# Wide query-key products for two blocks, values ahead of the second softmax, and outputs added by accumulating DMA, in a fused attention and gated-MLP layer

## The chip, the cores and the metric

The kernel runs on one core of a Trainium2 chip. Such a core has five engines with an instruction queue each: TensorE (PE in the profile) for matrix products, VectorE (DVE), ScalarE (ACT), GpSimd (POOL) and SyncE (SP). Each engine works through its instructions in order, and engines wait for each other by semaphores. SP's queue carries nearly all transfers here; GpSimd issues those that add to their destination. PSUM, where matmul results land, has eight banks of 128 x 512 fp32. The metric is the time of one execution on the device in microseconds (us), the median over runs.

## The reference

```python
B, S, D = 1, 2048, 640;  H = 32;  Dh = 20;  W, dil = 8, 2;  F = 1536
xn = _layernorm(x)
qkv = xn @ wqkv                                   # q, k, v: 32 heads of 20
idx = pos[:, None] - off[None, :]                 # off = 0, 2, ... 14
logits = jnp.einsum("bhsd,bhswd->bhsw", q, kg) * scale     # 8 keys per query
logits = jnp.where(mask[None, None, :, :], logits, -1e9)
attn = _softmax(logits, axis=-1)
o = jnp.einsum("bhsw,bhswd->bhsd", attn, vg)
h = (xn @ w_gate) * (xn @ w_up)                   # no activation between
return x + o.reshape(B, S, D) @ wo + h @ w_down
```

All inputs and the output are bf16. The two branches, attention over eight dilated positions and the gated product, read the same normalised x.

## The kernel before

The 2048 rows are 16 tiles of 128 for the layer norm (`front`) and four blocks of 512, j = 0 to 3, for everything else. D = 640 is five chunks of 128, F = 1536 is twelve. The normalised x is kept transposed (XNT), by TensorE for the first four tiles and by transposing DMA for the others.

Projections (L655, L687) give q (QT) and k (KT) with channels on partitions, and v, which is stored to DRAM (`v_scratch`) and read back shifted. A chunk of 128 channels holds four channels of each of the 32 heads.

Query-key products: for a block, DVE multiplies q with eight shifted views of k. `narrow` does four shifts of one chunk in one instruction (128 x 2048 bf16, L819) into a slot PRD. TensorE then sums over the channels of a head with a 0/1 matrix G, four 32-column matmuls per slot (L930, in `logits`), ten slots per block: two halves of the shifts (r = 1, 0) times five chunks. For a block in `QUAD`, four of the five chunks go another way (`wide`): DVE multiplies q straight from PSUM with two shifts of one chunk in fp32 (128 x 1024, L864), and the four chunks are added before TensorE sees them. Of those additions (`sum32`, `close`), the ones in `BY_DMA` are DMAs that GpSimd issues with an add at the destination (L886, 512 KB in SBUF), the others are GpSimd's own (L890, L908). Then four slots go to TensorE instead of ten. Before the change only block 3 is in `QUAD`.

Softmax runs for two blocks at a time (`softmax(x)`, x = 0 for blocks 0 and 1, x = 1 for 2 and 3) on DVE and ScalarE; its last step is L981. Then SP moves the result in 16 small DMAs (32 partitions of 4 x 256 B each, `move`) to ATX, where partitions are the channels of a chunk.

Weighted values: 20 units (block, chunk). For a block, ScalarE first copies two parts of ATX to two PSUM banks (L1076, `at_copy`). A unit's shifted v comes as four DMAs into one of four buffers VX; DVE multiplies VX with the two banks (L1091, fp32, slots PV), GpSimd adds pairs (L1096), TensorE sums the rest with a 0/1 matrix SEL (L1144) in batches of units (`BATCH`), and ScalarE evacuates to OT.

Gated product: for block j and each of 12 steps m, TensorE makes gate and up in two PSUM banks (L1195, five matmuls each), ScalarE copies the gate to SBUF (L660, tiles HT, HX or XNT), and DVE multiplies with up from PSUM (L1204), or ScalarE copies up too (UX) and GpSimd multiplies (L1221). A gate's bank is free once ScalarE has copied it.

Down and output: per tile of 128 rows two pieces of 320 columns, 12 matmuls over F and 5 over the attention's channels (L1277); DVE adds x (XR, loaded again) and writes FOUT (L1290), which SP stores.

The order is not written by hand. Each of these steps is a Python generator that yields tasks and conditions, and `Sched` places them greedily by its own durations: each engine's instruction order is fixed when the program is built, with a priority per task, a count of free PSUM banks, and waits only on the data itself. `calm` keeps GpSimd's additions out of the time in which a softmax runs on DVE.

Of the kernel before, what the change touches and what calls it, by code (L numbers as in the profile page):

```python
# [20 lines left out]
NJ = 4  # L21
# [327 lines left out]
def build_kernel(nc, A_x, A_wqkv, A_wo, B_x, B_w_gate, B_w_up, B_w_down, out):  # L349
# [42 lines left out]
    SV += [sb(f"SV{5 + i}", [128, 4, JB], at=a_ra + i * 4096) for i in range(3)]  # L392
    sv_free = list(range(NS))
# [21 lines left out]
    QUAD = {3: (1, 0)}  # L415
    BY_DMA = (((0, 0), (0, 2)), ((1, 0), (1, 2)))
    NXR = 3
    a_xr = place[0]
    XR = sb("XR", [128, NXR, D])
    FOUT = sb("FOUT", [128, 2, D])  # L420
# [17 lines left out]
    def ht(j, m):  # L438
        if j == 3:
            return XNT[:, m % NCH, m // NCH * JB:(m // NCH + 1) * JB]  # L440
        return HX[HXM[m]][:] if j == 2 else HT[:, j, m, :]
# [21 lines left out]
    def dma(o, i, r=(), w=(), name="", eng="sp", group=None, land=None):  # L463
# [10 lines left out]
       r=[IDENT[:]], w=[IDENT[:]], name="ident", occ=0.4)  # L474
    op("pool", lambda e: e.memset(G[:], 0.0), w=[G[:]], name="g0", occ=0.2)
# [43 lines left out]

    def late_loads():  # L520
        yield num(NJ, "lg")

        def go():
            src = B_w_down.rearrange("(c p) n -> p c n", p=128)
            dma(WD[:], src, w=[WD[:]], name="ld_wd")
            wo_src = A_wo.rearrange("(h d) n -> h d n", d=DH)
            for dq in range(4):
                a = WO[32 * dq:32 * dq + 32]
                dma(a, wo_src[:, dq:DH:4, :], w=[a], name=f"ld_wo{dq}", group="wo")

        yield have("vx", NVX - 1)
        yield Task("sp", go, prio=30)

    def front(t):
# [11 lines left out]

        def sqrt():
            op("act", lambda e: e.activation(sd, mv[:, 1:2], ACT.Sqrt, bias=EPSC[:, 0:1]), r=[("mv", t), EPSC[:]],  # L548
               w=[("sd", t)], name=f"sd{t}", occ=0.25)
            mark("sd", t)  # L550

        def recip():
            op("dve", lambda e: e.reciprocal(rstd, sd), r=[("sd", t)], w=[("rstd", t)], name=f"rstd{t}", occ=0.16)
            mark("rstd", t)
            if t >= N_DVE_A:
                op("dve", lambda e: e.tensor_scalar(nmr, mv[:, 0:1], rstd, -1.0, op0=ALU.mult, op1=ALU.mult),
                   r=[("mv", t), ("rstd", t)], w=[("nmr", t)], name=f"nmr{t}", occ=0.13)
# [27 lines left out]
        yield Task("act", sqrt, r=[("mv", t)], prio=p - 1)  # L585
        yield Task("dve", recip, r=[("sd", t)], prio=p)
# [192 lines left out]
    def calm():  # L779
        return all(("sm", x) in done or count.get(("logits", x), 0) < 2 for x in range(2))  # L780
# [10 lines left out]
    def products():  # L791
        rows = {j: [] for j in range(NJ)}
        holds = {}
        for j, kind in ORDER:
            if kind == "w":
                if j not in holds:
                    yield from fetch(j, 0, holds.setdefault(j, {c: [] for c in range(4)}))
                yield from wide(j, rows[j], holds[j])
            else:
                if len(QUAD.get(j, ())) == 2 and j not in holds:  # L800
                    yield from fetch(j, 0, holds.setdefault(j, {c: [] for c in range(4)}))
                for r in (1, 0):
                    for c in range(NCH - 1 if r in QUAD.get(j, ()) else 0, NCH):
                        yield from narrow(j, r, c, rows[j])
            if len(rows[j]) == 10 - 3 * len(QUAD.get(j, ())):
                K.spawn(logits(j, rows[j]))

# [17 lines left out]
    def q_bank(j, c, hold):  # L825
# [7 lines left out]
        def copy():  # L833
            evac([(QT[:, j, c, :], PS[:, hold[0], :], JB)], f"qev{j}_{c}")
            for _ in range(4):
                bump("qk", 0, j, c)
# [11 lines left out]
    def wide(j, slots, hold):  # L848
        halves = [(r, q0) for r in QUAD[j] for q0 in (0, 2)]
        acc, parts = {}, {1: [], 0: []}  # L850
        for c0 in (0, 2):
            for i, (r, q0) in enumerate(halves):
                f = []
                for c in (c0, c0 + 1):
                    yield lambda: len(hold[c]) > 0 and len(usable(j)) > 0
                    k = slot(j)
# [6 lines left out]
                    def go(o=o, qb=qb, kv=kv, q=q, rk=rk):  # L863
                        X = op("dve", lambda e: e.tensor_tensor(o[:], qb, kv, ALU.mult), r=[q, rk], w=[o[:]],  # L864
# [92 lines left out]
    def softmax(x):  # L957
        def tt(o, a, b, f, name, occ):
            return Task("dve", lambda: op("dve", lambda e: e.tensor_tensor(o, a, b, f), r=[a, b], w=[o], name=name, occ=occ,
                                          lock=True), r=[a, b], w=[o], prio=10, lock=True)  # L960
# [8 lines left out]
        def sub():  # L969
            op("dve", lambda e: e.tensor_tensor(L[:], L[:], bc(M3[:], 8), ALU.subtract), r=[L[:], m3], w=[L[:]], name="lsub",  # L970
               occ=1.2, lock=True)

        def exp():
            op("act", lambda e: e.activation(L[:], L[:], ACT.Exp), r=[L[:]], w=[L[:]], name="exp", occ=1.9)

        def recip():
            op("act", lambda e: e.activation(s3, s3, ACT.Ln), r=[s3], w=[s3], name="rln", occ=0.4)
            op("act", lambda e: e.activation(R, s3, ACT.Exp, scale=-1.0), r=[s3], w=[R], name="rs", occ=0.4)

        def attn():  # L980
            op("dve", lambda e: e.tensor_tensor(L[:], L[:], bc(RS[:], 8), ALU.mult), r=[L[:], R], w=[L[:], ("tok", x)], name="attn",  # L981
               occ=1.2, lock=True)

# [8 lines left out]
        yield num(2, "logits", x)  # L992
        if x:
            yield have("sm", x - 1)
# [16 lines left out]
    BATCH = (1, 4, 9, 14, 19)  # L1011

    def vx_loads():
        yield num(NJ, "lg")
# [24 lines left out]
    def weighted():  # L1039
# [5 lines left out]
        yield Task("act", take, banks=2, prio=0, contig=True)  # L1045
        for u in range(NU):
            yield from unit(u)

    def unit(u):
# [7 lines left out]
        yield lambda: len(sv_free) > 0  # L1057
# [15 lines left out]

        def at_copy(r):
            o, i = PS[:, at_bank[r], :], ATX[j // 2][:, j % 2, r, :]
            op("act", lambda e: e.activation(o, i, ACT.Copy), r=[i], w=[o], name=f"atp{j}_{r}", occ=0.55)  # L1076
# [33 lines left out]
        if c in (0, NCH - 1):  # L1110
            for r in range(2):
                if c == 0:
                    yield Task("act", lambda: at_copy(r), r=[ATX[j // 2][:, j % 2, r, :]],
# [20 lines left out]
    def sums(us):  # L1134
        hold = []
        for u in us:
            yield have("add", u)

# [24 lines left out]
    def on_pool(j, m):  # L1163
        return ("sm", 1) in done and m < 11 and ucount[0] - count.get(("hp",), 0) < HP_MAX

    def gu(j):
# [14 lines left out]
        for m in range(NF):  # L1181
# [5 lines left out]
            if j == 2 and m == 8:  # L1187
                yield have("atx", 1)
# [10 lines left out]
            def after(h=h, hold=hold, j=j, m=m):  # L1199
# [11 lines left out]
                if on_pool(j, m):  # L1211
# [16 lines left out]
                    yield calm  # L1228
# [9 lines left out]
    def xr_loads():  # L1238
        yield have("xnt", NT - 1)
        yield have("vx", NVX)  # L1240
        for t in range(NT):
            if t >= NXR:
                yield have("out", t - NXR)
            yield Task("sp", lambda: dma(XR[:, t % NXR, :], xhbm[t * TS:(t + 1) * TS, :], w=[XR[:, t % NXR, :]], name=f"xr{t}"),
                       prio=15, w=[XR[:, t % NXR, :]])
# [4 lines left out]
    def dn(j):  # L1250
# [3 lines left out]
        for st in range(4):  # L1254
            t = 4 * j + st
            pieces = ((0, 320), (320, 480), (480, 640)) if t == NT - 1 else ((0, 320), (320, 640))
            yield have("xr", t)
# [4 lines left out]
    def dn_piece(j, t, nb, rows, c0, c1):  # L1262
# [4 lines left out]
        o, xr = FOUT[:, t % 2, cols], XR[:, t % NXR, cols]  # L1267
# [25 lines left out]

        def store():
            if t == NT - 1:
                f, d = o, ohbm[t * TS:(t + 1) * TS, cols]
            else:
                f, d = FOUT[:, t % 2, :], ohbm[t * TS:(t + 1) * TS, :]
            stores.append(dma(d, f, r=[f], name=f"odma{t}_{nb}", eng="act" if nb == 1 and t == NT - 1 else "sp"))

        def tail():
            yield num(NCH, "ot", j)
            yield Task("pe", rest, r=[OT[:, j, :, rows]], prio=40)
            yield Task("dve", fin, r=[PS[:, hold[0], :], xr], w=[o], prio=FIN_PRIO)
# [7 lines left out]

    N_PE_T = 4
    BN_AFTER = (4,)
    N_DVE_A = 6
# [5 lines left out]
    ORDER = ((0, "n"), (1, "n"), (2, "n"), (3, "n"), (3, "w"))  # L1321
# [18 lines left out]
    def misc():  # L1340
        yield have("xnt", NT - 1)

        def sel():
            for q in range(4):
                a, b = SEL[32 * q:32 * q + 32, :], IDENT[32 * q:32 * q + 32, 32 * q:32 * q + 32]
                op("dve", (lambda a, b: lambda e: e.tensor_copy(a, b))(a, b), r=[b], w=[a], name=f"sel{q}", occ=0.1)

# [4 lines left out]
        yield Task("dve", sel, prio=19)  # L1352
# [57 lines left out]
```

## Time and profile before

| what | us |
| --- | --- |
| runs: median (lowest to highest of 3) | 268.62 (268.61 to 268.77) |
| profiled execution | 268.34 |
| its span, first to last instruction | 266.8 |
| TensorE busy | 261.3 |
| VectorE busy | 218.3 |
| GpSimd busy | 132.4 |
| ScalarE busy | 107.6 |

The span is a little shorter than the execution, which includes the start and the end. The busy times are of one execution. TensorE is busy for nearly all of the span at a granted clock of 1.00; its matmuls follow each other at 0.215 us for 512 columns. Lines name the place in the kernel that issued an instruction; ScalarE's copies out of PSUM share one line, so that they are told apart by the tile they write. A wait is put down to whatever came last of what the instruction needed.

### The profile page before, as it was taken

How to read it: one execution, taken by the hardware profiler on the slowest of the kernel's cores; microseconds unless marked ns; L12 is line 12 of the kernel's file. 1: busy time of each engine (PE TensorE's matmuls, PEld its weight loads, DVE VectorE, ACT ScalarE, POOL GpSimd, SP SyncE). 2: the span in 40 equal slices, each digit the busy share in tenths (PEclk: the TensorE clock that was granted, in tenths of full speed). 3: DMA queues.
4: the chain of work that ended last, by engine and by line, in shares of the span. 5: the costliest groups of instructions: out<-in, count | busy, mean ns of one | idle time of the engine just before them, and what ended most of it. 6: DMA issues, size and time to landing. Idle time of an engine off the chain costs nothing.

```text
span 266.8 us, 4468 instructions
## 1 busy us (share of the span) xinstructions
PE 261.3 (98%) x1771; PEld 152.6 (57%) x1788; DVE 218.3 (82%) x278; ACT 107.6 (40%) x193; POOL 132.4 (50%) x83
## 2 busy tenths in 40 slices
PE   7999999999999999999999999999999999999996
PEld 5996965444444444444444446764577547754775
DVE  4678899999999996379999899988998999981221
ACT  3469998556732122255434442007500460016000
POOL 1000000000007359700399999977999799979000
PEclk9999999999999999999999999999999999999999
DMA  7974789502226997193426733656345633130101
GB/s 213 374 207 81 195 107 371 213 0 98 101 49 161 192 234 178 9 333 81 114 49 142 170 80 87 185 162 168 80 129 152 184 96 89 49 98 2 49 27 49
DMA packets 40933, 35.75 MB, mean 134 GB/s; under 512 B 16080, under 2 KB 39120, under 8 KB 40912
## 3 DMA queue, kind: packets, MB, share of 16 engines
q1 hardware_dynamic: 40096, 33.31, 46.0%
q0 software_dynamic: 576, 2.10, 4.1%
q8 instruction: 14, 0.23, 0.4%
q10 hardware_dynamic: 240, 0.05, 0.1%
q14 instruction: 7, 0.06, 0.1%
HBM read 25.07 MB, written 5.26 MB: 114 GB/s over the span
## 4 chain that ended last, share of the span: by engine, by line
PE 96%; DVE 1%; DMA 1%; issue 1%; ACT 0%
PE PS L1195 39%; PE PS L1277 28%; PE PS L655 22%; PE PS L930 3%; PE PS L687 2%; PE PS L1144 2%; DMA XST<-in_A_x_dram 1%; PE PS L599 0%; DVE STATS L542 0%; ACT XNT L611 0%; DVE XNS L563 0%; DVE XNT L609 0%; DVE FOUT L1290 0%; ACT SD L548 0%; DVE MV L545 0%
## 5 line engine op out<-in xcount | busy, mean ns | idle before, releaser
L1096 POOL TENSOR_TENSOR SV<-PV 128x1024 bf16<-128x1024 f32 x40 | 93.2, 2361 | 20.4 <-DVE LOG L981 19.4
L1091 DVE TENSOR_TENSOR PV<-VX,PS 128x1024 f32<-128x1024 bf16 (+1 forms) x56 | 91.9, 1669 | 2.5 <-POOL SV L1096 2.3
L655 PE MATMUL PS<-XNT,WQKV 128*128 128x512 bf16 (+2 forms) x384 | 60.2, 315 | 0.4 <-issue 0.2
L1195 PE MATMUL PS<-XNT,WG 128*128 128x512 bf16 x238 | 59.4, 379 | 0.2
L1195 PE MATMUL PS<-XNT,WU 128*128 128x512 bf16 x231 | 57.7, 379 | 0.4 <-issue 0.2
L655 PEld LDWEIGHTS PS<-XNT,WQKV 128*128 128x128 bf16 x390 | 37.9, 112 | 21.8 <-ACT LOG L941 0.8
L1195 PEld LDWEIGHTS PS<-XNT,WG 128*128 128x128 bf16 x240 | 23.3, 98 | 28.5 <-issue 0.8
L1195 PEld LDWEIGHTS PS<-XNT,WU 128*128 128x128 bf16 x240 | 23.4, 98 | 28.2 <-ACT LOG L941 0.4
L819 DVE TENSOR_TENSOR PRD<-QT,KT 128x2048 bf16<-128x2048 bf16 x32 | 36.8, 1215 | 0.0
L1290 DVE TENSOR_TENSOR FOUT<-PS,XR 128x320 bf16<-128x320 f32 (+1 forms) x33 | 15.7, 477 | 18.4 <-PE PS L1277 18.3
L1277 PE MATMUL PS<-WD,HT 128*128 128x320 bf16 x192 | 28.5, 299 | 0.0
L660 ACT ACTIVATE HT<-PS 128x512 bf16<-128x512 f32 x24 | 14.3, 596 | 31.6 <-PE PS L1195 31.6
L1277 PE MATMUL PS<-WO,OT 128*128 128x320 bf16 (+1 forms) x165 | 26.6, 295 | 0.0
L890 POOL TENSOR_TENSOR PRF<-PRF,PRF 128x1024 f32<-128x1024 f32 x4 | 9.4, 2348 | 31.2 <-DVE PRF L864 31.2
L660 ACT ACTIVATE UX<-PS 128x512 bf16<-128x512 f32 x14 | 8.4, 597 | 39.5 <-PE PS L1195 39.5
L949 POOL MEMSET LOG<- 32x6 bf16 (+6 forms) x7 | 0.4, 96 | 47.6 <-ACT LOG L941 47.6
L1204 DVE TENSOR_TENSOR HT<-HT,PS 128x512 bf16<-128x512 bf16 x23 | 15.7, 684 | 9.5 <-PE PS L1195 7.4
L1277 PEld LDWEIGHTS PS<-WD,HT 128*128 128x128 bf16 x192 | 18.6, 98 | 8.0 <-issue 0.4
L1277 PEld LDWEIGHTS PS<-WO,OT 128*128 128x128 bf16 x165 | 15.9, 98 | 5.9
L864 DVE TENSOR_TENSOR PRF<-PS,KT 128x1024 f32<-128x1024 f32 x16 | 19.0, 1216 | 0.3 <-DMA PRF<-PRF 0.3
L660 ACT ACTIVATE XNT<-PS 128x512 bf16<-128x512 f32 x12 | 7.2, 598 | 25.5 <-PE PS L1195 25.5
L542 DVE BATCH_NORM_STATS2 STATS<-XST 128x6 f32<-128x320 bf16 x32 | 14.6, 472 | 2.5 <-DMA XST<-in_A_x_dram 2.5
(62 smaller groups left out, 235.7 us busy)
## 6 DMA issues: line engine op xcount, KB each, us to landing
VX<-v_scratch SPq DMA_DIRECT2D x80, 130.0 KB, 2.9
XST<-in_A_x_dram SPq DMA_DIRECT2D x16, 160.0 KB, 5.7
v_scratch<-VST SPq DMA_DIRECT2D x4, 640.0 KB, 4.2
XR<-in_A_x_dram SPq DMA_DIRECT2D x16, 160.0 KB, 2.7
out_dram<-FOUT SPq DMA_DIRECT2D x15, 160.0 KB, 1.8
PRF<-PRF POOLq DMA_DIRECT2D x4, 512.0 KB, 8.7
WG<-in_B_w_gate_dram SPq DMA_DIRECT2D x1, 1920.0 KB, 8.6
WU<-in_B_w_up_dram SPq DMA_DIRECT2D x1, 1920.0 KB, 12.0
```

The costliest lines, as they stand in the source:

```text
L542: op("dve", lambda e: e.bn_stats(o, a), r=[a], w=[("st", t, i)], name=f"bn{t}_{i}", occ=0.49)
L655: op("pe", (lambda o, l, x, c, first: lambda e: e.matmul(o, l, x, start=first, stop=(c == NCH - 1)))(o, l, x, c, first), r=[l, x], w=[o], ...
L660: X = op("act", (lambda o, i: lambda e: e.activation(o, i, ACT.Copy))(o, i), r=[i], w=[o], name=name, occ=0.12 + n * 0.9e-3)
L819: op("dve", lambda e: e.tensor_tensor(s[:], qb, kv, ALU.mult), r=[q, rk], w=[s[:]], name=f"prod{j}_{r}_{c}", occ=1.15, lock=True)
L864: X = op("dve", lambda e: e.tensor_tensor(o[:], qb, kv, ALU.mult), r=[q, rk], w=[o[:]], name=f"prow{j}_{r}_{c}_{q0}", occ=1.17)
L890: yield Task("pool", lambda: op("pool", lambda e: e.tensor_tensor(x, x, y, ALU.add), r=[x, y] + tokens(), w=[x], name=name, occ=2.36, lock ...
L1091: op("dve", lambda e: e.tensor_tensor(p, vw, a, ALU.mult), r=[vv] + rk, w=[p], name=f"pv{u}_{x}_{r0}", occ=0.09 + 1.1 * nr)
L1096: X = op("pool", lambda e: e.tensor_tensor(o, p[:, :, 0, :], p[:, :, 1, :], ALU.add), r=[p[:]] + tokens(), w=[o], name=f"pva{u}_{x}", occ= ...
L1195: op("pe", (lambda l, x, c: lambda e: e.matmul(PS[:, b, :], l, x, start=(c == 0), stop=(c == NCH - 1)))(l, x, c), r=[l, x], w=[PS[:, b, :] ...
L1204: X = op("dve", lambda e: e.tensor_tensor(h, h, PS[:, hold[1], :], ALU.mult), r=[h, PS[:, hold[1], :]], w=[h], name=f"h{m}_{j}", occ=0.65)
L1277: op("pe", (lambda l, x, i: lambda e: e.matmul(dst, l, x, start=(i == 0), stop=(i == n - 1)))(l, x, i), r=[l, x], w=[PS[:, b, :]], name=f" ...
L1290: X = op("dve", lambda e: e.tensor_tensor(o, PS[:, b, 0:wid], xr, ALU.add), r=[PS[:, b, :], xr], w=[o], name=f"fin{t}_{nb}", occ=0.15 + wi ...
```

## The change

- Block 2 joins block 3 in `QUAD`: eight of its ten narrow products become sixteen wide ones, added over four chunks by GpSimd and by four more accumulating DMAs. The order of the products is blocks 0 to 3 narrow, then 2 wide, then 3 wide.
- VX loads may start once all products are placed, not only when block 3's logits are. The two copies of ATX for block 0 are tasks of their own that may be placed as soon as ATX for blocks 0 and 1 has been moved, and the first units' buffers (SV, PV) are chosen so that units can run ahead of the second softmax. The last four gate results of block 2 go to a part of OT.
- `calm` becomes `room`: GpSimd may work within a softmax where its addition ends by the planned end of the softmax step then running, plus 0.3.
- Outputs of blocks 0 to 2: x is copied to the output in DRAM once (one DMA on SP), ScalarE copies the down results to SBUF, and GpSimd issues one DMA per block that adds 128 x 4 x 640 bf16 to the output. Block 3 goes as before, with x loaded once into four buffers.
- Square root, reciprocal and the small product of the layer norm are made for pairs of tiles from tile 4 on. SEL is made by GpSimd at the start rather than by DVE. The sums of the values come in seven batches instead of five.

```diff
-    SV += [sb(f"SV{5 + i}", [128, 4, JB], at=a_ra + i * 4096) for i in range(3)]
-    sv_free = list(range(NS))
+    SV += [sb("SV5", [128, 4, JB], at=a_ra + 6 * D * 2)]
+    sv_free = [3, 4, 0, 1, 2]
...
-    QUAD = {3: (1, 0)}
+    QUAD = {2: (1, 0), 3: (1, 0)}
     BY_DMA = (((0, 0), (0, 2)), ((1, 0), (1, 2)))
-    NXR = 3
-    XR = sb("XR", [128, NXR, D])
-    FOUT = sb("FOUT", [128, 2, D])
+    FB0 = sb("FB0", [128, 5, D])
+    FB1 = sb("FB1", [128, 2, D], at=a_ra)
+    XR = sb("XR", [128, 4, D], at=a_ra + 2 * D * 2)
...
-        return HX[HXM[m]][:] if j == 2 else HT[:, j, m, :]
+        if j == 2:
+            return OT[:, 3, m - 8, :] if m >= 8 else HX[HXM[m]][:]
+        return HT[:, j, m, :]
...
+    op("pool", lambda e: e.memset(SEL[:], 0.0), w=[SEL[:]], name="sel", occ=0.1)
+    for q in range(4):
+        op("pool", (lambda q: lambda e: e.affine_select(SEL[:], SEL[:], pattern=[[-1, 32]], compare_op=ALU.not_equal, fill=1.0,
+                                                        base=-32 * q, channel_multiplier=1))(q),
+           r=[SEL[:]], w=[SEL[:]], name=f"sel{q}", occ=0.2)
...
+        def copy_x():
+            a, b = ohbm[0:3 * JB, :], xhbm[0:3 * JB, :]
+            o, i = a.rearrange("(p r) n -> p (r n)", p=128), b.rearrange("(p r) n -> p (r n)", p=128)
+            op("sp", lambda e: e.dma_start(o, i), w=[("outx",)], dma=True, name="outx", nbytes=2e6)
+
+        yield num(2, "lg")
+        yield t(copy_x)
...
+        ts = next((g for g in GROUPS if t in g), (t,))
+        t0, t1 = ts[0], ts[-1] + 1
         def sqrt():
-            op("act", lambda e: e.activation(sd, mv[:, 1:2], ACT.Sqrt, bias=EPSC[:, 0:1]), r=[("mv", t), EPSC[:]],
-               w=[("sd", t)], name=f"sd{t}", occ=0.25)
-            mark("sd", t)
+            o, i = SD[:, t0:t1, 0:1], MV[:, t0:t1, 1:2]
+            op("act", lambda e: e.activation(o, i, ACT.Sqrt, bias=EPSC[:, 0:1]), r=[("mv", k) for k in ts] + [EPSC[:]],
+               w=[("sd", k) for k in ts], name=f"sd{t}", occ=0.25)
+            for k in ts:
+                mark("sd", k)
...
+            o, i = SD[:, t0:t1, 1:2], SD[:, t0:t1, 0:1]
+            op("dve", lambda e: e.reciprocal(o, i), r=[("sd", k) for k in ts], w=[("rstd", k) for k in ts], name=f"rstd{t}", occ=0.16)
...
+                n, m = SD[:, t0:t1, 2:3], MV[:, t0:t1, 0:1]
+                op("dve", lambda e: e.scalar_tensor_tensor(n, m, -1.0, o, op0=ALU.mult, op1=ALU.mult),
+                   r=[x for k in ts for x in (("mv", k), ("rstd", k))], w=[("nmr", k) for k in ts], name=f"nmr{t}", occ=0.13)
+            for k in ts:
+                mark("rstd", k)
...
-    def calm():
-        return all(("sm", x) in done or count.get(("logits", x), 0) < 2 for x in range(2))
+    def room(occ, ready=0.0):
+        def f():
+            if count.get(("logits", 0), 0) >= 2 and ("sm", 0) not in done:
+                return False
+            return due[0] == INF or max(K.t["pool"], K.t_lock, ready) + occ <= due[0] + SLIP
+
+        return f
+
+    calm = room(2.36)
...
-                if len(QUAD.get(j, ())) == 2 and j not in holds:
+                if len(QUAD.get(j, ())) == 2 and j not in holds and (j, "w") == ORDER[at + 1]:
...
+        mark("products")
...
-    BATCH = (1, 4, 9, 14, 19)
+    BATCH = (1, 4, 6, 9, 11, 14, 19)
...
     def vx_loads():
-        yield num(NJ, "lg")
+        yield have("products")
...
         yield Task("act", take, banks=2, prio=0, contig=True)
+        for r in range(2):
+            yield Task("act", lambda: at_copy(0, r), r=[ATX[0][:, 0, r, :]], w=[PS[:, at_bank[r], :]], prio=1)
         for u in range(NU):
             yield from unit(u)
+
+    def at_copy(j, r):
+        o, i = PS[:, at_bank[r], :], ATX[j // 2][:, j % 2, r, :]
+        op("act", lambda e: e.activation(o, i, ACT.Copy), r=[i], w=[o], name=f"atp{j}_{r}", occ=0.55)
...
-        yield lambda: len(sv_free) > 0
+        yield lambda: len(sv_free) > 0 and (sv_free[0] in (3, 4) or count.get(("lg",), 0) >= NJ)
...
-        if c in (0, NCH - 1):
+        if c == NCH - 1 or (c == 0 and j):
             for r in range(2):
                 if c == 0:
-                    yield Task("act", lambda: at_copy(r), r=[ATX[j // 2][:, j % 2, r, :]],
+                    yield Task("act", lambda: at_copy(j, r), r=[ATX[j // 2][:, j % 2, r, :]],
                                w=[PS[:, at_bank[r], :]], prio=1)
...
+        if us[-1] >= 3 * NCH:
+            yield num(8, "dn", 2)
...
-        return ("sm", 1) in done and m < 11 and ucount[0] - count.get(("hp",), 0) < HP_MAX
+        return count.get(("lg",), 0) >= NJ and m < 11 and ucount[0] - count.get(("hp",), 0) < HP_MAX
...
-            if j == 2 and m == 8:
-                yield have("atx", 1)
...
-                    yield calm
+                    yield room(1.15)
...
-        yield have("xnt", NT - 1)
-        yield have("vx", NVX)
+        yield num(8, "dn", 0)
+        for st in range(4):
...
-        o, xr = FOUT[:, t % 2, cols], XR[:, t % NXR, cols]
+        F, ft = (FB1, t % 2) if j == 3 else (FB0, t % 4)
+        o, xr = F[:, ft, cols], XR[:, t % 4, cols]
...
+        def fin_act():
+            K.free_bank(hold[0], evac([(o, PS[:, hold[0], 0:wid], wid)], f"fin{t}_{nb}"))
+            bump("fin", j)
+            if count["fin", j] == 8:
+                K.one(Task("pool", add_out, r=[F[:, 0:4, :]], prio=5))
+
+        def add_out():
+            d = ohbm[j * JB:(j + 1) * JB, :].rearrange("(t p) n -> p t n", p=128)
+            f = F[:, 0:4, :]
+            stores.append(op("pool", lambda e: e.dma_start(d, f, accum_op=ALU.add), r=[f, ("outx",)], w=[("out", j)], dma=True,
+                             name=f"oadd{j}", occ=0.88, acc=4))
...
+            if j < 3:
+                yield Task("act", fin_act, r=[PS[:, hold[0], :]], w=[o], prio=6)
+                return
...
+    SLIP = 0.3
+    GROUPS = ((4, 5), (6, 7), (8, 9), (10, 11), (12, 13), (14, 15))
-    ORDER = ((0, "n"), (1, "n"), (2, "n"), (3, "n"), (3, "w"))
+    ORDER = ((0, "n"), (1, "n"), (2, "n"), (3, "n"), (2, "w"), (3, "w"))
...
-        def sel():
-            for q in range(4):
-                a, b = SEL[32 * q:32 * q + 32, :], IDENT[32 * q:32 * q + 32, 32 * q:32 * q + 32]
-                op("dve", (lambda a, b: lambda e: e.tensor_copy(a, b))(a, b), r=[b], w=[a], name=f"sel{q}", occ=0.1)
...
-        yield Task("dve", sel, prio=19)
```

## The prediction

> **What bounds the kernel now.** I read the busy times first, then the chain that ended last, then the waits of TensorE, and only then the stretch from 70 to 112 us, because the order of the changed kernel's instructions puts new waits there.
>
> The first part of the page, and the fourth, the chain's shares by engine:
>
> ```profile
> PE 261.3 (98%) x1771; PEld 152.6 (57%) x1788; DVE 218.3 (82%) x278; ACT 107.6 (40%) x193; POOL 132.4 (50%) x83
> ...
> PE 96%; DVE 1%; DMA 1%; issue 1%; ACT 0%
> ```
>
> TensorE (PE) is busy for 98% of the span and is 96% of the chain. From 8.46 us to the last matmul at 264.25 it does not stop. So time can be won only by giving it less to do, and any wait that reaches it is lost in full. All of its waits in the list (microseconds in total, times, longest):
>
> ```profile
> PE PS L639 <- DVE ZERO L469: 1.3, 1, 1.3
> PE PS L687 <- DVE XNT L609: 0.3, 1, 0.3
> PE PS L655 <- issue: 0.2, 1, 0.2
> PE PS L1195 <- issue: 0.2, 1, 0.2
> ```
>
> The chain in order of time (start, length, what), around the logits of block 2:
>
> ```profile
> 76.74 2.27 PE PS L930 x40
> 79.01 0.16 issue
> 79.17 7.50 PE PS L1195 x34
> 86.67 2.16 PE PS L655 x10
> ```
>
> Forty group-sum matmuls take 2.27 us, 0.0568 each, and the switch back to full-width matmuls shows as 0.16. Then the transfers. The timeline of the SP queue and of GpSimd (POOL):
>
> ```profile
> 72.21 10.40 SPq L467 DMA_DIRECT2D ATX<-LOG  x16
> 82.66 0.59 SPq L467 DMA_DIRECT2D v_scratch<-VST  x1
> 83.37 10.34 SPq L467 DMA_DIRECT2D VX<-v_scratch  x16
> ...
> 86.96 1.01 POOL L886 DMA_DIRECT2D PRF<-PRF  x1 [1.34 <-DVE PRF L864]
> ...
> 96.07 0.86 POOL L886 DMA_DIRECT2D PRF<-PRF  x1 [2.00 <-DVE PRF L864]
> ```
>
> and the times from issue to landing, min/median/max, in the answers for the tiles ATX, VX and PRF, in this order:
>
> ```profile
> DMA to landing us min/median/max: 1.9/1.9/2.4
> ...
> DMA to landing us min/median/max: 2.3/2.9/15.0
> ...
> DMA to landing us min/median/max: 8.1/8.7/8.9
> ```
>
> The accumulating transfers (PRF, 512 KB each) take 8.1 to 8.9 us. The four were issued at 86.96, 90.04, 93.21 and 96.07 and landed at 95.06, 98.95, 101.83 and 104.90. The VX loads that were still queued in that stretch took up to 15.0 us instead of 2.9: units 2 and 3 landed at 105.16 and 106.67, just behind the last accumulation. The trace's packets say why. From 91.2 to 103.2 us some 45 accumulating packets of 4 KB (327 ns each) started per us, which fills 16 engines, and the SP queue got 52 VX packets per us beside them; once they were through it got 200. [...]
>
> **The change, part by part.** The sum is made against the profiled execution, 268.34 us (span 266.8 and 1.5 around it); the median of the three runs is 268.62, 0.28 more.
>
> Fewer group sums. Block 2's products come as 4 tiles instead of 10, so 24 of its 40 matmuls go: 24 x 0.0568 = -1.36 us, all of it on TensorE. The sums of the values are made in seven batches instead of five; each batch is a switch there and back, and the rows that show switches have 0.05 to 0.16 us for one: two batches cost 0.2 to 0.6, I take 0.3. Net -1.06.
>
> DVE. Eight narrow products of 1.22 us become sixteen wide ones of 1.22: +9.7. The 24 adds of x of blocks 0 to 2 go to ScalarE's copies: 24 x 0.487 = -11.7. GpSimd multiplies ten gate results instead of fourteen, DVE four more: 4 x 0.68 = +2.7. Four SEL copies go (-0.7), and six reciprocals of 0.16 and five small products of 0.21 (-2.0). About -2 in sum, on an engine at 82%; nothing of it reaches TensorE by itself. ScalarE gets 24 copies of about 0.5 us and is at 40%: hidden by its idle time, 31.6 us of which stand before the HT copies alone. If that cover went, it would be banks freed late, which is what follows below. The pairing of the square roots moves the first transpose's issue back by about one tile's 1.2 us; the transposes of tiles 4 and 5 landed at 19.8 and 21.3, and the matmuls that read them start near 24, which hides it.
>
> Copy of x to the output (2 MB, DRAM to DRAM) on SP's queue: issued in a stretch where the slices show DMA at 0 to 2 tenths; it stands ahead of two value stores and 10 us or more ahead of the ATX moves. The nearest row, the 1.9 MB load of WU, took 12.0 us; nothing asks for the copy before the first output. Cost 0.
>
> Values ahead of softmax 2. This is the part that decides. The two copies of ATX to PSUM (L1076, 0.60 us each) for block 0 now stand on ScalarE directly behind the second HT copy, ahead of the third; before, sixteen HT copies lay ahead of the first. ScalarE runs in order, so these copies wait for all 16 ATX moves, and every gate copy waits behind them. TensorE notices when it has no bank: two hold ATX, two hold the queries of block 2, which the wide products read from PSUM, and the gate and up results of steps 2 and 3 fill the other four. The gate matmuls of step 4 need the bank that the third HT copy frees.
>
> When TensorE gets there: before, the work at 79.17 us was all projections but ten matmuls, logits 0 to 2 and one gate group. In the changed order, ahead of step 4's gate, block 2's logits are missing (-2.27 - 0.16), ten more projections (-2.16), and seven more groups of five at 0.2158 are in it (+7.55): 79.17 + 2.96 = 82.1 us.
>
> When ATX is there: softmax 1's last product ended at 72.2; DVE is full from 60 to 80 us and has 2.7 us less to do before it (SEL, reciprocals, small products), so 69.5. The 16 issues take from 69.55 to 79.35 (9.8 between first and last, as in the row). Alone, the last lands 1.9 later, at 81.3. A semaphore, the two copies and the HT copy, 0.05 + 1.17 + 0.6 = 1.82: the bank is free at 83.1, a wait of 1.0 us. That is the lower end.
>
> But block 2's accumulations are now in the same stretch. GpSimd starts at the same 69.55 with two adds of 2.35 and issues the first at 74.25; in the trace the packets follow 3.4 us after the issue and are dense after 4.2, so from 78.45. The other three are issued, by DVE's order, before the third HT copy matters to it. By then, 8.9 us after the first issue, 1536 of ATX's 2048 packets had gone in the trace. The other 512, at 52 per us, take 9.8 us: 88.25, and 0.35 to the landing, 88.6. The upper end is the last accumulation's landing: 74.25 + 8.1 + 3 x 3.28 = 92.2. So the wait is 88.6 + 1.82 - 82.1 = 8.3 us, between 1.0 and 11.9; I take 8.3, since the row of VX is the nearest to it, small packets on the same queue beside the same accumulations.
>
> [...]
>
> Output by accumulating transfers. Three issues on GpSimd, 4 x 1280 B per partition each, which is 512 pieces where PRF has 128. Issuing PRF took 0.87 us at the median; the bounds are 0.87 and four times that, 3.5. From softmax 2's last product to the last value add, GpSimd has 34 adds of 2.32, six products of 1.12 and these three: 88.2 us at the lower bound. TensorE has 49 groups (52.9), 408 down matmuls (55.7), 60 sums and their switches (4.4): 113.0 between block 3's logits and that batch. That leaves 24.8 for softmax 2, whose rows and the products between them on DVE add to 19.2; the products also wait for GpSimd's buffers, so I take half of the 5.6 as cover, 2.8. I take 1.5 us per issue, under the cover, cost 0: the piece count is no row of the trace, the 0.87 is. Upper end 3 x 2.63 - 2.8 = +5.1.
>
> In sum: 268.34 - 1.36 + 0.3 + 8.3 = 275.6 us.
>
> **The rivals.** First, ATX is not held up (short packets pass in groups): wait 1.0, 268.34 - 1.06 + 1.0 = 268.3. For it: ATX's packets are 256 B and take 18 ns; against it, VX's 15.0. Second, the other side, faster: TensorE never waits, because the moves land by 80.3 or a bank more is free at step 4; then only the matmuls count, 267.3. It decides if ATX lands before 82.1 - 1.82 = 80.3, 1.0 us earlier than the last issue and the shortest landing allow. Third, GpSimd becomes a second bound through the output issues: 275.6 + 5.1 = 280.7; it starts above 1.8 us per issue.
>
> **How the numbers follow.** Forecast 0.68, with its own range 270.7 (SP gets twice the packets, 512 at 104 per us, landing at 83.7, wait 3.4) to 279.2 (landing at 92.2); not held up 0.11; faster 0.08; GpSimd as well 0.13, 277 to 284. From 270.5 to 281 lie nearly all of the first and two thirds of the last, about 0.8. About 0.2% (0.54 us) is what a measurement of this kernel tells from no change, 268.08 to 269.16: not held up gives same 0.08 and slower 0.03; in all faster 0.08, same 0.08, slower 0.84.
>
> **What would show it.** Right: a wait of ScalarE's ATX copy on the ATX transfer of 6 to 13 us in one piece, ATX's landings up to 10 us, a single wait of TensorE of about 8 us near 82 us at L1245, and an unbroken TensorE after it; 112 group-sum matmuls instead of 136. Wrong: ATX landing 1.9 us after its issues beside the accumulations; TensorE waiting instead before the value sums of the last block (GpSimd late), where the row of the output issue on POOL tells its length.

## The result and the profile after

The changed kernel took 282.06 us in the median (280.63 to 282.35 in four runs), the kernel before 268.69 beside it: a ratio of 1.0485, 95% interval 1.0447 to 1.0522. It is slower, by 13 us where I had forecast 7, and 1.1 us above the upper end of the range. The profiled execution is the shortest of the four: 280.63 us, span 278.8.

Busy times, and the shares of the chain that ended last:

```profile
PE 262.9 (94%) x1747; PEld 151.8 (54%) x1764; DVE 221.1 (79%) x249; ACT 111.8 (40%) x203; POOL 155.6 (56%) x99
...
PE 65%; DVE 14%; SPq 6%; ACT 5%; POOL 4%; DMA 3%; issue 2%; DVEq 0%
```

TensorE now stands for 15.9 us of the span instead of 5.5. The waits of TensorE (us in total, times, longest) have two rows that were not there:

```profile
PE PS L1245 <- ACT HT L686: 8.3, 1, 8.3
PE PS L1196 <- POOL SV L1146: 1.8, 1, 1.8
```

The first is the wait of the forecast, to the tenth. The timeline shows its two ends, ScalarE's second gate copy and the copies of ATX (start, length; in brackets the idle time and who ended it), and SP's sixteen moves:

```profile
77.09 0.60 ACT L686 ACTIVATE HT<-PS 128x512 bf16<-128x512 f32 x1 [3.72 <-PE PS L1245]
89.03 1.12 ACT L1101 ACTIVATE PS<-ATX 128x512 f32<-128x512 bf16 x2 [11.34 <-DMA ATX<-LOG]
...
69.10 17.51 SPq L469 DMA_DIRECT2D ATX<-LOG  x16
```

and, in the answers for the tiles ATX and PRF, issue to landing:

```profile
DMA to landing us min/median/max: 1.9/2.0/7.1
...
DMA to landing us min/median/max: 4.4/5.2/7.2
```

The moves landed at 89.0 (forecast 88.6), but not in the way I had it: their issues alone stretched from 10.40 to 17.51 us, and only 3.8 us lie between the start of the last issue (85.23) and the landing. (The second line of landings covers all eight accumulations; those of block 2, beside the moves, took 5.3 to 7.2 us.) What I had not seen at all stands in the table of stretches. The columns are the stretch, its length, the busy times of the five engines, the granted clock, the DMA share and GB/s:

```profile
82.00:88.00 6.00, 0.45 (x3) 0.00 (x0) 0.00 (x0) 0.00 (x0) 0.34 (x1) 0.90 1.05 199
88.00:91.00 3.00, 0.28 (x1) 0.13 (x2) 0.30 (x1) 1.97 (x4) 0.00 (x0) 0.50 1.04 287
91.00:92.00 1.00, 1.00 (x4) 0.32 (x3) 1.00 (x2) 0.15 (x1) 0.00 (x0) 0.50 1.05 236
92.00:93.00 1.00, 1.00 (x4) 0.42 (x3) 1.00 (x2) 0.00 (x0) 0.40 (x1) 0.50 1.07 250
93.00:94.00 1.00, 1.00 (x5) 0.35 (x3) 0.11 (x1) 0.60 (x1) 1.00 (x1) 0.66 1.11 212
94.00:95.00 1.00, 1.00 (x7) 0.41 (x6) 0.40 (x1) 0.00 (x0) 0.94 (x1) 1.00 1.09 223
```

While TensorE stood (its last matmul ended at 82.45), its clock fell to half at 86.86, and it stayed there beyond the restart at 90.72 to 93.68 (a mean of 0.66 in the fifth row is 0.68 us at half): 2.96 us in which half of the work was done, 1.5 us lost. The trace's clock record gives 6.83 us at 0.5 in all, and a mean of 0.988 over the span. The other three runs had 0.982: 0.018 x 280.5 / 0.5 = 10.1 us at half, one stretch of 3.4 us more, which costs 1.7 us under work. That is about the distance from 280.63 to the other three, 281.82 to 282.35, of which no trace was kept.

The sum, against the profiled execution before (us):

| term | forecast | measured |
| --- | --- | --- |
| 24 group-sum matmuls | -1.36 | -1.3 |
| two more batches of sums | +0.3 | +0.4 |
| TensorE's wait for the ATX copies | +8.3 | +8.3 |
| half clock after it | 0 | +1.5 |
| wait for a value tile, at 177 us | 0 | +2.2 |
| first full-width projections at 8.78, not 8.46 | 0 | +0.3 |
| a gate bank at 162 us | 0 | +0.2 |
| sum | +7.2 | +11.6 |

The whole is 280.63 - 268.34 = 12.3; 0.7 us are not accounted for. (Rows one and two are from the experiments; the value tile's wait is 1.8 us in its row and 2.21 between matmul starts.)

### The profile page after: what moved, and what is told of

Its sections match the earlier page's. It is cut to its first block, busy times and chain, and to the rows that moved or that the text cites. A ratio compares the mean times of both kernels' runs of the same rounds, so it can differ in the third digit from the quotient of the medians.

```text
span 278.8 us, 4404 instructions
## 1 busy us (share of the span) xinstructions
PE 262.9 (94%) x1747; PEld 151.8 (54%) x1764; DVE 221.1 (79%) x249; ACT 111.8 (40%) x203; POOL 155.6 (56%) x99
## 4 chain that ended last, share of the span: by engine, by line
PE 65%; DVE 14%; SPq 6%; ACT 5%; POOL 4%; DMA 3%; issue 2%; DVEq 0%
PE PS L1327 27%; PE PS L1245 26%; PE PS L681 8%; SPq L469 6%; DVE PRD L856 4%; POOL SV L1146 3%; ACT XNS L592 3%; DVE SM L999 2%; DVE PV L1141 2%; PE PS L713 2%; PE PS L1196 2%; DMA XST<-in_A_x_dram 1%; DMA ATX<-LOG 1%; PE PS L969 1%; DVE PRF L903 1%
## 5 line engine op out<-in xcount | busy, mean ns | idle before, releaser
L1146 POOL TENSOR_TENSOR SV<-PV 128x1024 bf16<-128x1024 f32 x40 | 96.5, 2674 | 12.5 <-DVE LOG L1026 7.8
L1141 DVE TENSOR_TENSOR PV<-VX,PS 128x1024 f32<-128x1024 bf16 (+1 forms) x54 | 90.9, 1729 | 6.9 <-POOL SV L1146 6.9
L1245 PE MATMUL PS<-XNT,WU 128*128 128x512 bf16 x236 | 59.2, 381 | 0.4 <-issue 0.3
L903 DVE TENSOR_TENSOR PRF<-PS,KT 128x1024 f32<-128x1024 f32 x32 | 37.9, 1217 | 0.3 <-PE PS L681 0.3
L929 POOL TENSOR_TENSOR PRF<-PRF,PRF 128x1024 f32<-128x1024 f32 x8 | 18.8, 2358 | 32.0 <-DVE LOG L1026 20.7
L1254 DVE TENSOR_TENSOR HT<-HT,PS 128x512 bf16<-128x512 bf16 x24 | 16.4, 685 | 17.9 <-ACT HT L686 9.5
L856 DVE TENSOR_TENSOR PRD<-QT,KT 128x2048 bf16<-128x2048 bf16 x24 | 27.3, 1222 | 0.0
L686 ACT ACTIVATE FB<-PS 128x320 bf16<-128x320 f32 x24 | 10.5, 438 | 40.1 <-PE PS L1327 40.1
L947 POOL TENSOR_TENSOR PRD<-PRF,PRF 128x1024 bf16<-128x1024 f32 x8 | 18.7, 2357 | 1.6 <-DVE PRF L903 1.6
L1340 DVE TENSOR_TENSOR FB<-PS,XR 128x320 bf16<-128x320 f32 (+1 forms) x9 | 4.1, 455 | 15.4 <-PE PS L1327 15.4
```

The lines of the kernel that those rows point to most:

```text
L686: X = op("act", (lambda o, i: lambda e: e.activation(o, i, ACT.Copy))(o, i), r=[i], w=[o], name=name, occ=0.12 + n * 0.9e-3)
L856: op("dve", lambda e: e.tensor_tensor(s[:], qb, kv, ALU.mult), r=[q, rk], w=[s[:]], name=f"prod{j}_{r}_{c}", occ=1.15, lock=True)
L929: yield Task("pool", lambda: op("pool", lambda e: e.tensor_tensor(x, x, y, ALU.add), r=[x, y] + tokens(), w=[x], name=name, occ=2.36, lock ...
L947: yield Task("pool", lambda: op("pool", lambda e: e.tensor_tensor(o, a, y, ALU.add), r=[a, y] + tokens(), w=[o], name=f"qend{j}_{r}_{q0}", ...
L1141: op("dve", lambda e: e.tensor_tensor(p, vw, a, ALU.mult), r=[vv] + rk, w=[p], name=f"pv{u}_{x}_{r0}", occ=0.09 + 1.1 * nr)
L1146: X = op("pool", lambda e: e.tensor_tensor(o, p[:, :, 0, :], p[:, :, 1, :], ALU.add), r=[p[:]] + tokens(), w=[o], name=f"pva{u}_{x}", occ= ...
```

## The experiments

**Is the early copy the loss, or a second bound behind it?** The two copies of ATX for block 0 go back to where the first values need them; the planner then puts them behind eighteen gate copies.

```diff
-        for r in range(2):
-            yield Task("act", lambda: at_copy(0, r), ...)
         for u in range(NU):
...
-        if c == NCH - 1 or (c == 0 and j):
+        if c in (0, NCH - 1):
```

> The change complete, but the two copies of ATX for block 0 are asked for where the first values need them, as before; the planner then puts them behind eighteen gate copies instead of two. Theory (ScalarE's wait for the ATX moves is the loss, and what comes after it is its consequence): no wait of TensorE at L1243 near 82 us, a granted clock of 1.00, and a time of 268.34 - 1.06 + 0.3 for the later first matmul = 267.6 us, or up to 269.4 if the 1.8 us wait for the value tile stays. The moves themselves still take long to issue (about 17 us), since the accumulations are where they were. Rival (GpSimd and DVE are a second bound that the wait only hid): the first wait goes, but TensorE waits for products or value tiles instead, and the time stays above 274 us.

Measured: 271.3 us (270.53 to 272.12), ratio 1.0099 (1.0068 to 1.0129), above the 269.4 that I had allowed. The 8.3 us are gone, though SP's issues still took 17.09 us: the moves may be late where nothing stands behind them. The half clock is gone in the profiled run and in one more; the other two (271.97 and 272.12 us) still had a clock of 0.994, one stretch. Of the waits of TensorE, this was the longest left:

```profile
PE PS L1196 <- POOL SV L1146: 1.8, 1, 1.8
```

So eleven of the thirteen us follow from where two copies of 0.6 us stand in ScalarE's queue. The rival falls, and a second loss remains.

**Is the half clock a consequence of standing idle?** The up matmuls just ahead of the wait are issued eight times, into the same bank.

```diff
-  op("pe", lambda e: e.matmul(PS[:, b, :], l, x, start=(c == 0), stop=(c == NCH - 1)), ...)
+  op("pe", lambda e: mm(e, again=7 if (which, m, j, c) == (1, 3, 0, 0) else 0), ...)
```

> The changed kernel, with the up matmuls of step 3 of block 0 (the last ones ahead of the 8.3 us wait) issued eight times instead of once into the same bank: 7 x 5 x 0.2158 = 7.55 us of matmuls in a time in which TensorE would wait. Theory (the half clock comes from TensorE standing idle): the remaining wait is about 0.8 us, the granted clock stays 1.00, and the time falls by what half clock cost after the wait, 1.5 to 3.2 us: 278.8 to 280.3 us. Rival (the clock falls for another reason, such as the transfers or the mere place): the clock stays at 0.98 to 0.99 and the time at 280.6 to 282.4 us.

Measured: 279.92 us (278.77 to 280.75). In the timeline of TensorE the matmuls fill the wait, and the clock stays at 1.00 there (five matmuls in 1.24 us):

```profile
81.25 7.72 PE L1249 MATMUL PS<-XNT,WU 128*128 128x512 bf16 x35
88.81 1.24 PE L1250 MATMUL PS<-XNT,WU 128*128 128x512 bf16 x5
90.90 1.25 PE L1250 MATMUL PS<-XNT,WG 128*128 128x512 bf16 x5 [0.84 <-ACT HT L686]
```

7.55 us of needless matmuls made the kernel 2.1 us faster in the median. Two of its runs had a clock of 1.00 (278.77 and 279.17) and two 0.994 (280.67 and 280.75). In the profiled one, one of the latter, the half clock comes elsewhere, after the second wait:

```profile
177.00:178.00 1.00, 0.10 (x2) 0.10 (x2) 1.00 (x2) 0.00 (x0) 1.00 (x2) 1.00 0.30 49
178.00:179.00 1.00, 1.00 (x4) 0.28 (x3) 1.00 (x2) 0.58 (x1) 1.00 (x2) 0.54 0.92 255
179.00:180.00 1.00, 1.00 (x4) 0.30 (x3) 1.00 (x2) 0.02 (x1) 1.00 (x1) 0.50 0.90 234
180.00:181.00 1.00, 1.00 (x5) 0.49 (x4) 1.00 (x1) 0.33 (x1) 1.00 (x1) 0.50 0.47 101
181.00:182.00 1.00, 1.00 (x7) 0.65 (x6) 1.00 (x2) 0.26 (x1) 1.00 (x2) 0.76 0.67 199
```

By these rows the half clock lasted 0.92 + 1 + 1 + 0.48 = 3.40 us.

**The same without any transfer.** In the kernel before, the gate of step 4 waits for multiplies on GpSimd that nothing else needs; nine of them, and then four.

```diff
                     K.free_bank(hold[0], evac([(h, PS[:, hold[0], :], JB)], f"gev{m}_{j}"))
+                    if (m, j) == (3, 0):
+                        for k in range(9):          # or 4
+                            op("pool", <UX = XNT * XNT, 128x512>, r=[("go",)], w=[u, ("stall",)])
...
-                       r=[l, x], w=[PS[:, b, :]], name=f"gu{which}_{m}_{j}_{c}"
+                       r=[l, x] + ([("stall",)] if (which, m, j, c) == (0, 4, 0, 0) else []), ...
```

> The kernel before, with the gate matmuls of step 4 of block 0 made to wait for nine extra multiplies on GpSimd (1.15 us each, 10.35 in all, from the copy of step 3 on; TensorE gets there some 2.4 us after that copy). No transfer is added. Theory (any idle time of this length halves the clock): TensorE waits about 8 us, the clock then shows 0.98 to 0.99, and the time is 268.7 + 8 + 1.5 to 3.2 = 278.2 to 279.9 us. Rival (the clock fell because of the accumulations beside it): the clock stays 1.00 and the time is 276.7 us.

> The kernel before, with the gate matmuls of step 4 of block 0 made to wait for four extra multiplies on GpSimd (4.6 us) instead of nine: TensorE stands for 8.5 - 5 x 1.15 = 2.8 us. Theory (the clock goes by stretches of 3.41 us on a time base of its own, since all stretches of half clock so far lasted 3.41, 6.83 or 10.24 us; one mostly idle stretch halves it): 271.5 us without a lost stretch and 273.2 with one, and runs of both kinds, since 2.8 us of idle time may or may not fill most of one. Rival (only a wait longer than a whole stretch lowers the clock): all runs 271.5 us with a clock of 1.00.

Measured with nine: 279.74 us (279.11 to 280.08), clock 0.982 in every run: 0.018 x 277.6 / 0.5 = 10.0 us at half in the profiled one. The matmuls behind the wait ran at half speed, ten in 4.1 us where the next ten took 2.2:

```profile
97.55 2.32 PE L1195 MATMUL PS<-XNT,WG 128*128 128x512 bf16 x5 [8.54 <-POOL UX L1206]
99.66 2.11 PE L1195 MATMUL PS<-XNT,WU 128*128 128x512 bf16 x5
101.61 1.24 PE L1195 MATMUL PS<-XNT,WG 128*128 128x512 bf16 x5
102.69 1.24 PE L1195 MATMUL PS<-XNT,WU 128*128 128x512 bf16 x5
```

With four, the wait was 2.4 us:

```profile
91.49 2.31 PE L1195 MATMUL PS<-XNT,WG 128*128 128x512 bf16 x5 [2.38 <-POOL UX L1206]
```

The runs fell into two kinds: 271.01 and 271.03 us with a clock of 1.00, 272.67 to 272.95 (four runs, the profiled one among them) with 0.994. So idle time alone does it here, with no transfer added. The time at half clock was 3.40 us with the filled wait, 6.83 in the changed kernel, 10.0 with nine multiplies and 0.006 x 271.2 / 0.5 = 3.3 with four: once, twice, three times and once about 3.4 us. A wait of 2.4 us cost one such stretch, 1.7 us, in four runs of six, and none in two. The rival, that only a wait longer than a stretch counts, falls. That the stretches keep a time base of their own, and that a mostly idle one sets the clock, was my theory; the runs show the lengths and both kinds of runs, not the cause.

**Do the accumulations hold up the ATX moves?** Those of block 2 are cut to 32 of the 1024 elements of a partition, then to 512; block 2's logits are then incomplete.

```diff
-  e.dma_start(x, y, accum_op=ALU.add)
+  e.dma_start(x[:, 0:1, 0:32], y[:, 0:1, 0:32], accum_op=ALU.add)    # or [:, 0:1, :]; j == 2 only
```

> The changed kernel, with the four accumulating transfers of block 2 cut to a 32nd of their bytes (64 of 2048 bytes a row; block 2's logits are then not summed over all chunks). Theory (these accumulations hold up the ATX moves): the sixteen ATX moves issue in about 10.4 us instead of 17.5, the last lands near 81.5, TensorE's wait at L1245 is 0.5 to 2 us instead of 8.3, the clock is 1.00, and the time is 268.34 - 1.06 + 0.3 + 1.2 = 268.8 us, up to 270.6 with the value tile's wait. Rival (the moves are slow for another reason: their own 256-byte pieces, the value loads, GpSimd's adds): issue 17 us, wait 8 us, 280 to 282 us.

> The changed kernel, with the four accumulating transfers of block 2 cut to half their bytes (512 of the 1024 elements of each partition; block 2's logits are then not summed over all chunks). Theory (the bytes of these transfers that the DMA engines move beside the ATX moves set the delay): midway between the 11.3 us and 17.5 us of issue, and the 1.0 and 8.3 us of wait, that a 32nd and the whole gave: issue 13.5 to 15 us, wait 3.5 to 5.5 us, 275 to 276 us without a stretch of half clock and up to 279 with some. Rival (they hold up the moves by being there, whatever their size above a little): issue and wait as with whole transfers, 280 us or more.

Measured with a 32nd: 271.67 us (271.37 to 273.57; the last at a clock of 0.994). The wait is as expected, the issue 0.9 us and the time 1.1 us above. The waits of TensorE and the timeline of SP:

```profile
PE PS L1197 <- POOL SV L1147: 1.8, 1, 1.8
...
PE PS L1246 <- ACT HT L686: 1.0, 1, 1.0
```

```profile
69.21 11.31 SPq L469 DMA_DIRECT2D ATX<-LOG  x16
```

With half: issue 12.26 and wait 1.9 in the profiled execution (272.58 us), less than my midway; the other three executions took 276.75 to 279.12 us with a clock of 0.982 to 0.988. That is more than the 1.7 us per stretch of half clock explain, so they probably waited longer; they left no trace. Between a 32nd and the whole (11.31 and 17.51 us of issue) the bytes matter; the law is not settled, and on half the size the experiment is inconclusive.

Not all of the longer issue goes with their bytes: with a 32nd the sixteen issues, 11.31 us, still take 0.9 us more than the 10.40 before. What holds SP there stays open.

**What is the second wait?** In the profile with late copies, the timelines of DVE and GpSimd (POOL) side by side in softmax 2:

```profile
135.71 2.78 DVE L999 TENSOR_TENSOR M<-M 128x512 bf16<-128x512 bf16 x2
...
145.86 3.04 DVE L999 TENSOR_TENSOR SM<-LOG 128x1024 f32<-128x1024 bf16 x1
148.93 1.98 DVE L999 TENSOR_TENSOR SM<-SM 128x512 f32<-128x512 f32 x2
...
135.15 2.73 POOL L1146 TENSOR_TENSOR SV<-PV 128x1024 bf16<-128x1024 f32 x1 [0.44 <-DVE PV L1141]
...
145.46 2.35 POOL L1146 TENSOR_TENSOR SV<-PV 128x1024 bf16<-128x1024 f32 x1
147.76 2.14 POOL L1271 TENSOR_TENSOR HX<-HX,UX 128x512 bf16<-128x512 bf16 x1
```

Three DVE steps are stretched, from 0.43 to 2.45, from 1.22 to 3.04 and from 0.69 to 1.53 us. They ended 0.28, 1.09 and 0.56 us after the GpSimd instruction beside it (which ended at 137.9, 147.8 and 149.9), so that most of its usual time lay behind that end. GpSimd's product, 1.15 us alone, took 2.14 in its turn and ended 1.0 us after the DVE step that ended at 148.9. `room` had placed these adds behind the maxima and behind the sums, but only in planned time: no semaphore holds GpSimd there, and in the execution it came early. In this experiment one does.

```diff
+        smx = [("smx",)] if x else []
-                X = op("dve", <softmax step>, r=[a, b], w=[o], ...)
+                X = op("dve", <softmax step>, r=[a, b], w=[o] + smx, ...)
...
-            X = op("pool", <value add>, r=[p[:]] + tokens(), w=[o], ...)
+            X = op("pool", <value add>, r=[p[:], ("smx",)] + tokens(), w=[o], ...)
-                        op("pool", <gate product>, r=[h, us], w=[h], ...)
+                        op("pool", <gate product>, r=[h, us, ("smx",)], w=[h], ...)
```

> The kernel with the late copies of ATX, in which GpSimd's value adds and gate products also wait for the steps of softmax 2 that were planned ahead of them (a semaphore where there was only a planned time). Theory (the remaining 2.2 us wait for a value tile comes from softmax 2: in the profile with late copies its rows on DVE are stretched from 0.43 to 2.45, from 1.22 to 3.04 and from 0.69 to 1.53 us, each beside a GpSimd instruction, 4.7 us in all): these rows go back to 0.43, 1.22 and 0.69, TensorE's wait at L1196 goes, no run has a clock below 1.00, and the time is 270.63 - 2.2 - 0.3 = 268.1 us, the same as before within 0.5. Rival (GpSimd's own work is what is late): the rows shrink, but GpSimd does its adds later, the wait stays near 2 us, and the time at 270.5 to 272 us.

Measured: 267.67 us (267.58 to 267.79), ratio 0.997 (0.9958 to 0.9982), clock 1.00 in all runs. The DVE groups by shape (busy, mean ns of one, idle before):

```profile
L999 DVE TENSOR_TENSOR SM<-LOG 128x1024 f32<-128x1024 bf16 x2 | 2.4, 1217 | 0.0
L999 DVE TENSOR_TENSOR SM<-SM 128x512 f32<-128x512 f32 x2 | 1.4, 692 | 0.1
...
L999 DVE TENSOR_TENSOR M<-M 128x512 bf16<-128x512 bf16 x2 | 0.8, 424 | 0.1
```

In the changed kernel their means were 2125, 1109 and 1440 ns. Softmax 2 is 2 x (0.91 + 0.42 + 1.02) = 4.7 us shorter (softmax 1, the other of each two, was undisturbed), no wait at L1196 is left, and GpSimd, which was held, is not late: its adds behind softmax 2 start at 153.2 instead of 157.7. All waits of TensorE that are left:

```profile
PE PS L665 <- DVE ZERO L471: 1.3, 1, 1.3
PE PS L625 <- DVE XNS L586: 0.4, 1, 0.4
PE PS L713 <- DVE XNT L635: 0.3, 1, 0.3
```

What did not stretch are the value products (PV<-VX,PS, with one input in PSUM): in the profile with late copies the one at 132.79, beside a GpSimd add, took 2.28 us, and so did the one at 150.83, with GpSimd idle. The steps that stretched (M<-M, SM<-LOG, SM<-SM) have no PSUM tile. The runs show that these steps and GpSimd's instructions delayed each other; why was not shown.

The same hold with the early copies left in:

> The changed kernel with its early copies of ATX, and GpSimd held to the planned order in softmax 2 as before. Theory (two separate losses): the wait of 8.3 us at L1245 and its half clock stay, the value tile's wait at L1196 goes with the 2.2 us and its share of half clock: 280.63 - 2.2 - 0.3 = 278.1 us where two stretches of half clock are lost and 279.8 where three are; if all runs have a clock of 0.988, the third stretch that the other runs of the changed kernel lost was that of the second wait. Rival (the second wait is only what the first leaves behind): 280.6 us or more with the wait still there.

Measured: 278.84 us (278.36 to 279.09). The second wait is gone and the first is there, so these are two losses:

```profile
PE PS L1245 <- ACT HT L686: 8.5, 1, 8.5
```

The clock was 0.981 to 0.982 in all runs (0.018 x 277.3 / 0.5 = 10.0 us at half in the profiled one): the first wait alone costs three stretches here. (With three, I had expected 279.8 us, 1.0 more.) Which wait the third stretch in the other runs of the changed kernel belongs to stays open.

**What are the intended gains worth?** Two edits of the kernel with late copies and held adds: five batches, and block 2's products as before.

```diff
-    BATCH = (1, 4, 6, 9, 11, 14, 19)
+    BATCH = (2, 6, 10, 14, 19)
```

> The same with the values' sums in five batches (after units 2, 6, 10, 14 and 19) instead of seven. Theory (a batch costs TensorE 0.09 us on the way in and 0.26 on the way out, as the gaps between matmul starts show in both profiles, and not the 0.15 that I took): 2 x 0.35 = 0.7 us less than the same kernel with seven, 267.4 us, faster than before by 0.4%. Rival (a batch costs 0.15, or larger batches wait for their last add): 267.8 us or more, or a new wait for a value tile.

```diff
-    QUAD = {2: (1, 0), 3: (1, 0)}
-    ORDER = ((0, "n"), (1, "n"), (2, "n"), (3, "n"), (2, "w"), (3, "w"))
+    QUAD = {3: (1, 0)}
+    ORDER = ((0, "n"), (1, "n"), (2, "n"), (3, "n"), (3, "w"))
```

> The same kernel with late copies and held adds, but the products of block 2 as before: ten tiles and 40 group sums, six of its chunk halves not added on GpSimd, no accumulating transfers for it. Theory (the products of block 2 are worth their 24 group-sum matmuls, 24 x 0.0568 = 1.36 us, and nothing else once the copies are late): 1.4 us slower than with them, 269.5 us. Rival (the accumulations beside the ATX moves and the added DVE work still cost something elsewhere): the same time or less than with them, 268.1 us or below.

Measured: 267.24 us (267.13 to 267.32), ratio 0.9953 (0.9941 to 0.9965), the fastest of all, and 268.96 us (268.73 to 269.39), ratio 1.0017 (1.0009 to 1.0026). Block 2's wide products are worth 268.96 - 267.67 = 1.29 us, close to the 1.36 of their 24 matmuls. Two batches cost 0.43 us, 0.21 each: more than my 0.15, less than the 0.35 that I then expected from the gaps at the switches alone. (These five batches end at other units than the five of the kernel before.)

The second time says one thing more. Without block 2's wide products the rest of the change, even with late copies and held adds, is 0.5 us slower than the kernel before, about what the two batches cost. So the 24 matmuls are all the gain that these runs show; the other parts of the change, none of which was measured alone, gain nothing together.

The accumulating outputs were not tried alone, nor taken out alone.

## Why the prediction was right and wrong

- **Group sums, -1.36 + 0.3**: right; 1.29 and 0.43.
- **DVE and ScalarE at nothing, the copy of x at nothing**: right, but for the 0.2 us wait for a gate bank that ScalarE freed late; the copy of x was issued at 40.4, landed 18.0 us later, and was over before the moves.
- **Values ahead of softmax 2, 8.3 us**: right in place, cause and size, and by luck in part. TensorE stopped at 82.45 (82.1 in the forecast) and the moves landed at 89.0 (88.6). But the step in between was wrong twice. The accumulating packets began 1.6 us after their first issue, and were dense at once, where I took 4.2; and from 75 to 87 us 79 ATX packets passed per us, not 52, beside 41 of theirs of 4 KB. (The 45 of the prediction counts 4-byte packets too; without them it was 42.) These two errors roughly cancel. The 79 is a mean of two kinds of time. Where the packets of one accumulation ran dense, at 45 to 49 per us, it was 17 per us (75.4 to 77.7 us), 30 (79.0 to 81.4), 39 (82.0 to 84.2) and 46 (85.0 to 87.2); where one accumulation ended and the next began, it was 199 (78.0 to 79.0), 283 (81.4 to 82.0) and 223 (84.2 to 85.0). So the 52 beside 45 that the forecast took over from the VX loads is near the last of these stretches, not the first, and the forecast had no such bursts. Also, I let SP issue at its old pace and put the whole delay behind the last issue, while SP itself was held.
- **How the DMA engines share the two queues**: not shown. Neither the 17 to 46 ATX packets per us beside dense accumulations nor the 199 to 283 between two of them follow from one ratio, and the forecast had used one, 52 to 45.
- **"An unbroken TensorE after it"**: this is the step that failed. Each term that I missed lies there: 1.5 us of half clock (3.2 where three stretches are lost) and the 2.2 us wait for a value tile. The trace of before could not show the first, as TensorE never stood there between its start and its last matmul; but a forecast of 8 us of idle time should have had a term for it, and the range's upper end, 281, had none. The second was in reach: the order showed GpSimd's adds inside softmax 2, and I asked only whether GpSimd had time for them, not whether a semaphore kept them to their time.
- **Outputs, 1.5 us per issue, cost 0**: right as far as the waits show; 1.2 to 1.6 us each. The third rival named the value sums as the place where GpSimd would be late, but by these issues. TensorE's wait for a value tile ended at 179.2, and the first of these issues came at 202.1.
- **The range**: it missed by 1.1 us. The direction, with a chance of 0.84, was right.

## What to carry to other kernels

Two copies that waited 11.3 us for a transfer kept the gate copies behind them in ScalarE's queue, and by them TensorE for 8.3: ask of each instruction that was moved how late its data can be, and who waits for the work behind it. Where TensorE is the bound and must stand, add the half clock after it to the wait: here a stretch of about 3.4 us cost up to 1.7 us, waits of 1.8 and 2.4 us cost one in some runs, and waits of 8.3 to 8.5 us cost two or three. A planned time is no order: GpSimd's adds came early in the execution and ran beside steps of softmax 2 that they were planned behind, and these became 4.7 us longer until a semaphore held them. What must not run beside something else needs one.

## What the runs showed that I had not expected

- Needless matmuls in a wait made the kernel faster (279.92 us instead of 282.06), which I came to expect only after the result.
- Sixteen issues on SP's queue took 17.5 us instead of 10.4 while four accumulating transfers of 512 KB ran from GpSimd's queue; cut to 16 KB each, they left it at 11.3.
- Those transfers landed in 5.3 to 7.2 us beside the 256 B moves, and in 8.1 to 8.9 beside the VX loads in the kernel before. Block 3's four in the changed kernel, from 112.7 us on and beside no other transfer, took 4.4 to 5.2.
